# A small first load moved from Sync's queue to ScalarE's, in a decode kernel of attention and a gated feed-forward

## Chip, cores and metric

The kernel runs on one core of one Trainium2 chip. The metric is the device time of one execution in microseconds (us).

## What is computed

Two tokens (B = 2) of width 512 pass through a layer norm. Its result feeds a sliding-window attention over a cache (32 heads of width 128, the last 2,048 of 8,192 positions) and a gated feed-forward of width 1,376 without a nonlinearity. Both are added to the input. The reference, cut:

```python
def _A_ref(x, k_cache, v_cache, wq, wo):          # W = 2048, Sk = 8192
    q = (x @ wq).reshape(B, 1, 32, 128).transpose(0, 2, 1, 3)
    k, v = k_cache[:, :, Sk - W:, :], v_cache[:, :, Sk - W:, :]
    p = softmax(einsum("bhqd,bhkd->bhqk", q, k) * 128 ** -0.5)
    o = einsum("bhqk,bhkd->bhqd", p, v)
    return o.transpose(0, 2, 1, 3).reshape(B, 1, 4096) @ wo
def _B_ref(x, w_gate, w_up, w_down):
    return ((x @ w_gate) * (x @ w_up)) @ w_down
xn = layernorm(x)
return x + _A_ref(xn, ...) + _B_ref(xn, ...)
```

All data is float32. Some 160 MB of cache and weights are read once per execution.

## The kernel before, in words

The host lays all weights and the used part of the cache out in one array, `stream`, in the order in which they are read. `blocks()` (its list ends with `out`) cuts this into a first small load, key `("f", 0)`, and the loads of the steps, key `("s", i)`. The small load holds the input `x`, two selection matrices `pick` and `rows`, and `w` 0, the columns of the query weights for head 0: 128 rows of 542 numbers. Load 0 holds the rest of the first four heads' query weights (`w` 1), K of heads 0, 1 and 2, and parts of later query weights. Load 1 holds the gate and up weights of the feed-forward and K of head 3; load 2 holds down weights, K of heads 4 and 5 and the first values V. Later loads hold K of one or two heads and V of heads some steps back.

Each step load goes into one of three slots of SBUF (`slots`, `BUFS` = 3). `pump()` (line 297) issues the next load whenever a slot is free, all of them on Sync's queue (`sp.dma_start`, line 316). It is called once before anything else, and then gives out the small load and loads 0, 1 and 2. After that `done()` (line 318) calls it when the last field of a slot has been used: load 3 follows when K of heads 0 to 2 and the weights beside it are used up, load 4 when load 1 is. After the first `pump()` Sync also issues `x_nat` (the input once more, for the last addition) and `carry` (a small matrix that is used near the end).

The small load is read first. VectorE (DVE), TensorE (PE) and ScalarE (ACT) make the layer norm of it: a sum, a matmul with `mean_w`, squares, a second sum and matmul, a square root on ScalarE, a reciprocal, the product `xn` and its copy over 128 columns, `xnb`. `project_first(0)` multiplies `xnb` with `w` 0 into `q_first`, the query of head 0, in the bank `tr`. `project_first(1)` does the same for heads 1 to 3 when load 0 has landed. Then the loop over the loads runs for each head `h`: `products(h)` multiplies K by the query on VectorE, in place; `sums(h)` adds up the products and gives K's slot back; `maxima`, `weights` and `reciprocals` make the softmax on VectorE, GpSimd and ScalarE; `values` multiplies by V on TensorE, and `project_o` and `down` add into one accumulator.

`Flow` records all operations in the order of the program and then writes them out, one list for each engine, with semaphores where one operation needs another. Engines run their lists in order. Every DMA has a semaphore of its own, which counts to 16. As `Flow.emit` records every operation, nearly all of them have one line, L243, in the profile, so tiles tell them apart: `first` is the small load, `step` the slots, `tr` and `q` the banks of the queries, `s` the scores.

Of the kernel before, what the change touches and what calls it, by code (L numbers as in the profile page):

```python
# [50 lines left out]
def pitch(fields):  # L51

    n = -(-sum(w for _, _, w in fields) // BLK)
    return (n | 1) * BLK
# [217 lines left out]
def sliding_attention_plus_glu_kernel(  # L272
# [7 lines left out]
    pe, dve, act, pl, sp = (flow.engine(unit) for unit in ("pe", "dve", "act", "pl", "sp"))  # L280
# [12 lines left out]
    tiles, used, left, got = {}, {}, {}, {}  # L293
# [3 lines left out]
    def pump():  # L297
        while todo:
            key, fields, at = todo[0]
            if key not in tiles:  # L300
                if key[0] == "f":
                    n = sum(w for _, _, w in fields)
                    tiles[key] = flow.tile([P, n], "first")
                elif not slots:
                    return
                else:
                    tiles[key] = slots.pop(0)
                used[key] = 0
            todo.pop(0)
            c0 = used[key]  # L310
            for kind, i, w in fields:
                got[kind, i] = (tiles[key][:, used[key] : used[key] + w], key)
                used[key] += w
            c1 = used[key]
            src = stream[at : at + P * pitch(fields)].rearrange("(p i) -> p i", p=P)
            sp.dma_start(tiles[key][:, c0:c1], src[:, : c1 - c0])

    def done(kind, i):
        _, key = got.pop((kind, i))
        left[key] -= 1  # L320
        if left[key] == 0 and key[0] != "f":
            slots.append(tiles.pop(key))
            pump()

    pump()
    xT = got["x", 0][0].rearrange("p (b c) -> p b c", b=B)
    pick = got["pick", 0][0].rearrange("p (r s b) -> p r s b", s=2, b=B)
# [494 lines left out]
```

## Time and profile before

| | |
|---|---|
| Median of 3 runs | 376.0 us (375.85 to 376.57) |
| Profiled execution, from its first to its last instruction (span) | 374.6 us |
| What the median has beyond that span | 1.4 us |
| HBM read | 159.47 MB, 426 GB/s over the span |
| Queue of the loads (q1) | 3,938 packets, 159.54 MB |
| Instruction queues (q8, q14) | 12 packets, 0.16 MB |
| TensorE, VectorE, ScalarE, GpSimd busy | 248.4, 295.1, 58.1, 25.3 us |

The page gives no other time of the profiled execution than its span; the runs that were timed are separate executions. The span begins with the first instruction that the profile shows and ends with the last. "DMA share" is the mean busy share of the core's 16 DMA engines. In windows a DMA packet is counted whole where it starts, so a window that is short beside a packet (some 2.3 us for a row of a large load) can show a share of nothing or of more than one. The time "to landing" of a DMA runs from its issue to the moment when the last of its 16 parts has arrived.

### The profile page before, as it was taken

The numbers are of one execution on the slowest core, as the hardware profiler recorded it, in microseconds if no ns is written. First come the engines' busy times: TensorE is split into PE (matmuls) and PEld (weight loads), VectorE is DVE, ScalarE is ACT, GpSimd is POOL, SyncE is SP. The second block draws the span as 40 slices with busy tenths as digits, with TensorE's granted clock in tenths as the row PEclk, the third lists the DMA queues.
The fourth block names the chain that finished last, engine by engine and source line by source line (L and its number), as shares of the span: only waits on it lengthen the run. The fifth ranks groups of instructions, "written<-read, shape, count | busy, mean of one in ns | idle before, by whom it ended". The sixth has DMA issues, their size and how long they took to land.

```text
span 374.6 us, 2741 instructions
## 1 busy us (share of the span) xinstructions
PE 248.4 (66%) x1094; PEld 86.8 (23%) x1094; DVE 295.1 (79%) x147; ACT 58.1 (16%) x259; POOL 25.3 (7%) x78
## 2 busy tenths in 40 slices
PE   3167675896578157855658585781488647476997
PEld 3033124231132013211212121320122112111344
DVE  3069998994599994599999945999999459999760
ACT  1002012111022012110202020300121201111232
POOL 1000000100001000000000000010001000000010
PEclk9759695898689758896969886998689868666999
DMA  8999999999999999999999999999999999999996
GB/s 345 420 465 454 450 432 435 434 434 424 427 427 434 434 434 434 436 434 441 434 435 429 434 434 434 434 429 434 434 435 434 429 434 434 428 426 416 414 432 250
DMA packets 3950, 159.70 MB, mean 426 GB/s; under 512 B 466, under 2 KB 610, under 8 KB 994
## 3 DMA queue, kind: packets, MB, share of 16 engines
q1 hardware_dynamic: 3938, 159.54, 98.6%
q8 instruction: 8, 0.13, 0.1%
q14 instruction: 4, 0.03, 0.0%
HBM read 159.47 MB, written 0.07 MB: 426 GB/s over the span
## 4 chain that ended last, share of the span: by engine, by line
DMA 64%; DVE 26%; PE 7%; ACT 1%; issue 0%; SPq 0%
DMA step<-in_stream_dram 64%; DVE s L243 13%; DVE step L243 13%; PE q L243 3%; PE acc L243 2%; PE o_ps L243 2%; PE tr L243 1%; ACT o_sb L243 0%; DVE m L243 0%; ACT oT L243 0%; DVE rec L243 0%; SPq L243 0%; DVE o_out L243 0%
## 5 line engine op out<-in xcount | busy, mean ns | idle before, releaser
L243 DVE TENSOR_TENSOR step<-step,q 128x4096 f32<-128x4096 f32 x31 | 136.8, 4411 | 47.0 <-DMA step<-in_stream_dram 47.0
L243 DVE TENSOR_REDUCE s<-step 128x32 f32<-128x4096 f32 x32 | 141.4, 4419 | 1.1
L243 PE MATMUL q<-step,xnb 128*128 128x512 f32 (+1 forms) x128 | 79.0, 759 | 80.5 <-DMA step<-in_stream_dram 80.5
L243 PE MATMUL o_ps<-step,p 128*16 128x512 f32 (+1 forms) x512 | 98.5, 730 | 11.2 <-DMA step<-in_stream_dram 11.2
L243 PEld LDWEIGHTS q<-step,xnb 128*128 128x128 f32 x128 | 28.0, 238 | 123.5 <-DMA step<-in_stream_dram 92.9
L243 PE MATMUL acc<-step,oT 128*9 128x512 f32 (+1 forms) x88 | 39.1, 604 | 8.7 <-ACT oT L243 8.7
L243 PE MATMUL tr<-first,o_sb 128*128 128x2 f32 (+2 forms) x198 | 29.1, 266 | 17.9 <-ACT o_sb L243 12.0
L243 PEld LDWEIGHTS tr<-first,o_sb 128*128 128x128 f32 x198 | 26.8, 205 | 40.6 <-ACT o_sb L243 31.3
L243 PEld LDWEIGHTS o_ps<-step,p 128*16 128x16 f32 x512 | 17.6, 107 | 78.6 <-issue 64.9
L243 ACT COPY o_sb<-o_ps 128x512 f32<-128x512 f32 (+1 forms) x24 | 13.8, 576 | 121.4 <-PE o_ps L243 121.4
L243 POOL PARTITION_ALL_REDUCE mm<-m x32 | 11.3, 355 | 268.6 <-DVE m L243 258.7
L243 ACT ACTIVATE nm<-mm 128x2 f32<-128x2 f32 x32 | 6.5, 203 | 148.0 <-POOL mm L243 148.0
L243 ACT ACTIVATE p<-s,nm 128x16 f32<-128x16 f32 x64 | 19.2, 300 | 1.0
L243 POOL PARTITION_ALL_REDUCE sum<-rs x32 | 12.7, 398 | 69.1 <-ACT p L243 69.1
L243 ACT ACTIVATE oT<-tr,rec 128x1 f32<-128x1 f32 x64 | 12.2, 260 | 27.0 <-PE tr L243 27.0
L243 DVE TENSOR_TENSOR step<-step,tr 128x4096 f32<-128x4096 f32 x1 | 4.4, 4422 | 14.8 <-DMA step<-in_stream_dram 14.8
L243 ACT ACTIVATION_READ_ACCUMULATOR p<-s,nm 128x1 f32 x64 | 11.9, 187 | 0.0
L243 PE MATMUL o_ps<-step,xn 128*2 128x512 f32 (+1 forms) x48 | 10.1, 548 | 0.0
L243 PEld LDWEIGHTS acc<-step,oT 128*9 128x9 f32 x88 | 4.6, 94 | 21.1 <-ACT oT L243 14.5
L243 DVE TENSOR_TENSOR o_out<-acc,x_nat 128x128 f32<-128x128 f32 x1 | 0.3, 292 | 8.4 <-PE acc L243 8.4
L243 DVE TENSOR_REDUCE m<-s 128x2 f32<-128x32 f32 x32 | 6.0, 186 | 1.1
L243 DVE RECIPROCAL rec<-sum 128x2 f32<-128x2 f32 x32 | 5.0, 155 | 1.9 <-POOL sum L243 1.9
(43 smaller groups left out, 41.5 us busy)
## 6 DMA issues: line engine op xcount, KB each, us to landing
step<-in_stream_dram SPq DMA_DIRECT2D x14, 7936.0 KB, 37.7
step<-in_stream_dram SPq DMA_DIRECT2D x2, 7680.0 KB, 32.0
step<-in_stream_dram SPq DMA_DIRECT2D x1, 7872.0 KB, 58.2
step<-in_stream_dram SPq DMA_DIRECT2D x1, 7808.0 KB, 38.8
step<-in_stream_dram SPq DMA_DIRECT2D x1, 4864.0 KB, 30.3
step<-in_stream_dram SPq DMA_DIRECT2D x2, 2304.0 KB, 19.6
step<-in_stream_dram SPq DMA_DIRECT2D x1, 2048.0 KB, 18.3
step<-in_stream_dram SPq DMA_DIRECT2D x1, 1024.0 KB, 19.8
```

What stands on the lines that cost most here:

```text
L243: made = getattr(eng, method)(*args, **kwargs)
```

## The change

In `pump()` the queue of a load is chosen by its key: the small load goes to ScalarE's queue (`act`), all others stay on Sync's.

```diff
             c1 = used[key]
             src = stream[at : at + P * pitch(fields)].rearrange("(p i) -> p i", p=P)
-            sp.dma_start(tiles[key][:, c0:c1], src[:, : c1 - c0])
+            queue = act if key[0] == "f" else sp
+            queue.dma_start(tiles[key][:, c0:c1], src[:, : c1 - c0])
```

Nothing else is changed. The small load is the first thing that the program writes for ScalarE, and load 0 is now the first thing that it writes for Sync. Tiles, sizes, semaphores and the order of all later work are as before.

## The prediction

> **What bounds the kernel now.** I read the page first: the busy shares, the slices of DMA and the chain of waits.
>
> ```profile
> span 374.6 us, 2741 instructions
> PE 248.4 (66%) x1094; PEld 86.8 (23%) x1094; DVE 295.1 (79%) x147; ACT 58.1 (16%) x259; POOL 25.3 (7%) x78
> DMA  8999999999999999999999999999999999999996
> DMA 64%; DVE 26%; PE 7%; ACT 1%; issue 0%; SPq 0%
> ```
>
> The DMA engines are in their top tenth from the second slice to the last but one. Whether that means "always full" is read from their share in long windows (columns: stretch, length, five engines, granted clock, DMA share, GB/s):
>
> ```profile
> 100.00:200.00 100.00, 65.47 (x255) 19.46 (x254) 87.64 (x38) 15.31 (x70) 6.77 (x18) 0.80 1.00 435
> 200.00:300.00 100.00, 65.61 (x266) 20.40 (x266) 82.14 (x39) 16.23 (x78) 7.53 (x20) 0.85 1.00 435
> ```
>
> The share is 1.00 at 435 GB/s. So the stream of loads sets the end, and the 26% that the chain gives to DVE lies beside full queues. A change matters here in two ways only: it moves the moment at which the big loads begin on the DMA engines, or it makes the engines lose time later. The start is where the change is:
>
> ```profile
> 0.72 1.28 ACT L243 ACT_TABLE_LOAD   x1 [0.72 <-PEq L804]
> 0.72 0.37 SPq L243 DMA_DIRECT2D first<-in_stream_dram  x1
> 1.15 1.37 SPq L243 DMA_DIRECT2D step<-in_stream_dram  x3
> 3.55 0.16 DVE L243 TENSOR_REDUCE st<-first 128x2 f32<-128x8 f32 x1 [0.74 <-DMA first<-in_stream_dram]
> 5.62 0.26 ACT L243 ACTIVATE st<-tr,eps_t 128x2 f32<-128x2 f32 x1 [3.62 <-PE tr L243]
> 7.07 3.42 PE L243 MATMUL tr<-first,xnb 128*128 128x128 f32 x16 [1.48 <-DVE xnb L243]
> 21.98 4.42 DVE L243 TENSOR_TENSOR step<-step,tr 128x4096 f32<-128x4096 f32 x1 [14.81 <-DMA step<-in_stream_dram]
> ```
>
> SP hands out the small load at 0.72 and load 0 (the K of heads 0 to 2) at 1.15. The small load is used from 3.55; layer norm and the first query are done at 7.07 + 3.42 = 10.49, and DVE then waits until 21.98 for load 0. That wait of 14.81 us is the cover for whatever happens to the small load.
>
> **The change part by part.** *The issue.* Load 0 is given out at 0.72 instead of 1.15, 0.43 us earlier, and loads 1 and 2, x_nat and carry move up with it. What this is worth depends on when the DMA engines turn to load 0. The windows and slices around that moment (40 slices of 0.99 us in the first line):
>
> ```profile
> GB/s 0 350 263 0 88 526 0 0 88 88 175 0 0 175 88 0 0 263 0 88 0 0 88 175 0 0 350 350 350 350 263 526 175 175 788 350 263 526 613 88
> 1.70:2.69 0.99, 0.00 (x0) 0.00 (x0) 0.88 (x3) 0.30 (x1) 0.08 (x3) 1.00 0.79 191
> 2.69:3.18 0.49, 0.00 (x0) 0.00 (x0) 0.11 (x1) 0.00 (x0) 0.00 (x0) 1.00 5.53 2188
> 5.10:5.80 0.70, 0.49 (x2) 0.40 (x2) 0.00 (x0) 0.18 (x1) 0.00 (x0) 1.00 3.25 1404
> ```
>
> A packet is booked where it starts. The small load's first packets appear in the second slice of 1.70 to 2.69, at 1.73, 1.0 us after their issue. Load 0's first 16, one for each engine, start in 2.69 to 3.18, on average at about 2.93; their issue at 1.15 plus the same 1.0 us would have allowed 2.15, so they queue behind the small load, not behind SP. The engines thus spend 2.93 - 1.73 = 1.20 us on a load of 271 KB (its row stands below), which at 435 GB/s takes 0.64 us. The other 0.56 us is the first packets' slow start. If load 0 comes first, the 0.64 us of bytes is still to be moved; the 0.56 us is gained in full if load 0's long packets hide the slow start, and not at all if load 0 suffers it itself. Gain: 0 to 0.56 us, and I take the middle, 0.28, as no row leans either way.
>
> *Two queues on the same engines.* The small load is 128 rows of 271 KB / 128 = 2,168 bytes, 8 for each of the 16 engines, now on ScalarE's queue while SP's queue is full of long packets. One load on one queue never shows what such alternation costs; the nearest rows are the few instruction packets that cut into the stream. Each row is one packet in a window of 0.02 us (first two) or 0.01 us, so its share times window times 16 is its time:
>
> ```profile
> q8 instruction: 1, 0.02, 290.0%
> q1 hardware_dynamic: 1, 0.06, 884.7%
> q14 instruction: 1, 0.01, 193.1%
> q1 hardware_dynamic: 1, 0.06, 1620.0%
> q1 hardware_dynamic: 1, 0.06, 1463.8%
> ```
>
> In order: the 16 KB packet at 51.43 (0.93 us), the load packet behind it at 52.35 (2.83 us), the 8 KB packet at 86.42 (0.31 us), the load packet behind it (2.59 us), and an undisturbed neighbour at 86.75 (2.34 us). The big cut cost 0.93 + 2.83 - 2.34 = 1.42 us for bytes that at 27.2 GB/s per engine (435 / 16) need 0.60: 0.82 us lost. The small one cost 0.31 + 2.59 - 2.34 = 0.56 for 0.30: 0.26 us lost. For 2,168 bytes the loss lies between nothing and 0.82 us, eight times over: 0 to 6.6 us. I take the row nearest in size, the 8 KB one, and scale by bytes, 0.26 x 2,168 / 8,192 = 0.07 us, because the loss grew with the packet: 8 x 0.07 = 0.55 us. A loss below nothing is excluded: engines at share 1.00 have no idle time that the alternation could fill.
>
> *The small load lands later.* The cut at 51.43 also shows how the queues take turns, for it falls in the middle of load 2 (between its start after the landing of load 1 and its own landing):
>
> ```profile
> step<-in_stream_dram SPq DMA_DIRECT2D x1, 7872.0 KB, 58.2
> step<-in_stream_dram SPq DMA_DIRECT2D x1, 7808.0 KB, 38.8
> step<-in_stream_dram SPq DMA_DIRECT2D x1, 7680.0 KB, 20.8
> first<-in_stream_dram SPq DMA_DIRECT2D x1, 271.0 KB, 2.8
> ```
>
> So a second queue gets its turn between two packets of one load. With turns one for one, each of the 8 small packets waits for one long one: 3.25 x 0.70 = 2.28 us (the window 5.10 to 5.80), plus 0.08 for its own bytes and the 0.07 above, 2.43 us; eight of them from 1.73 end at 21.2, landed by 21.5. From there to the first query it takes 10.49 - 3.55 = 6.94 us, so DVE's first product starts at 28.4 instead of 21.98, 6.5 us late. The next thing that could be late is load 3, which needs load 0's slot; then load 4, which needs load 1's:
>
> ```profile
> 48.95 0.36 SPq L243 DMA_DIRECT2D step<-in_stream_dram  x1
> 58.02 0.33 SPq L243 DMA_DIRECT2D step<-in_stream_dram  x1
> ```
>
> DVE frees the slot 48.95 - 21.98 = 26.97 us after its first product: now at 55.4, with packets 1.0 us later at 56.4. The engines run out of loads 0 to 2 (23,360 KB, 55.0 us at 435 GB/s, from 2.93) at 57.9. That leaves 1.5 us, so the lateness costs nothing; load 4 would be issued at 64.5, with a whole load still ahead of it. If that cover were gone, every us more would be a us of the end.
>
> *The rest.* ScalarE's table load (1.28 us) moves behind an issue of 0.37 us and ends near 2.4, long before 5.62: nothing, and 0.4 us of an already covered chain if it were not. No wait is added. x_nat and carry stay behind loads 0 to 2 and are used at the end. The last loads and what follows them are untouched.
>
> **Sum.** 374.6 - 0.28 + 0.55 = 374.9 us of span. The runs' median is 376.0, 1.4 us above the profiled span, and I keep that difference: **376.3 us**. The case's own range takes a gain of 0 to 0.56 and a loss of 0 to 1.0 us: 375.4 to 377.0. A measurement of this kernel tells about 0.2%, 0.75 us, from no change, so this case reads as "same".
>
> **The rivals.** *Every turn costs a full bubble (slower).* If the loss is a fixed time for each change of queue and not in proportion to bytes, eight turns cost 8 x 0.26 = 2.1 to 8 x 0.82 = 6.6 us on every engine: 376.0 - 0.28 + 2.1 = 377.8 to 382.3, the low end likelier because the 8 KB row is nearer. It decides from (0.75 + 0.28) / 8 = 0.13 us a turn. For it: both cuts cost more than their bytes. Against it: those packets go somewhere other than a load's do, the losses differ threefold, and successive loads on SP's queue show a share of 1.00.
>
> *Load 3 comes too late (slower).* If the small load's completion waits for a ninth long packet, it lands at 23.9, the slot is free at 57.8, packets come at 58.8, and the engines stand empty for 0.9 us; slower matrix work in the chain would add to that. 377.0 to 378. For it: only 1.5 us of slack. Against it: the fastest engine has the least slack, the others more.
>
> *The small load goes in one turn.* Then the engines change queue once instead of eight times, and the sum is 376.0 - 0.28 + 0.07 = 375.8, with the landing either near 3 or near 20 us. The cut in mid-load speaks against long turns of SP's queue, though not against long turns of short packets. The Trainium skill, in "DMA: Bandwidth & Descriptors", section "Queues, rings and completion order", says that an engine goes round its queues and drains a whole packet, typically 9 to 17 descriptors, before it switches; by that rule the eight would go together, and the cut in mid-load agrees with it only if a packet here holds fewer than eight long descriptors.
>
> *The small load is free (faster).* If its packets fit beside the long ones at no cost, load 0 starts 1.20 us earlier: 374.8. Against it: share 1.00 leaves no room beside.
>
> *The small load is not first on ScalarE.* If the table load stays ahead, its issue comes at 2.0 instead of 0.72, it lands later by about one turn, and load 0 still goes first. The slack above is mostly used; 376.0 to 376.6.
>
> **How the numbers follow.** Forecast 0.45, the bubble 0.20, one turn 0.15, free 0.10, load 3 late 0.07, table load first 0.03. Faster by over 0.2%: the free case and the edge of one turn, 0.13. Slower: the bubble, most of load 3 late, the edge of the forecast, 0.29. The rest, 0.58, is within. The range leaves out the upper half of the bubble and part of the free case: 375.1 to 378.2.
>
> **What would show it.** Right: load 0's packets near 1.73, the small load landing near 21, DVE's first product near 28, load 3 issued near 55 with the DMA share still 1.00 around 58, an end within 0.75 us. Wrong: load 0's packets of more than 2.4 us all through the first 20 us (bubbles), a window below 1.00 at 57 to 60 (load 3), or a small load that lands near 3 (no alternation), which would make the middle of the argument wrong even if the time holds.

## The result, and the profile after

The changed kernel takes 378.41 us (median of 5 runs, 377.88 to 378.80) against 376.26 us (375.85 to 376.57, 5 runs) before: a ratio of 1.0055 with a 95% interval of 1.0044 to 1.0066. It is 2.1 us slower, where 376.3 us and "no change" had been forecast, with a range of 375.1 to 378.2. The profiled execution of the changed kernel took 378.04 us with a span of 376.7.

The page's head, its DMA line and its queues:

```profile
span 376.7 us, 2741 instructions
DMA  8999999999999999999999999999999999999994
q1 hardware_dynamic: 3794, 159.26, 98.1%
q10 hardware_dynamic: 144, 0.28, 0.2%
```

The stream of loads is still what bounds the kernel; the small load has moved to a queue of its own, q10. The timeline of the start:

```profile
0.72 0.40 ACTq L243 DMA_DIRECT2D first<-in_stream_dram  x1
0.72 1.32 SPq L243 DMA_DIRECT2D step<-in_stream_dram  x3
1.15 1.28 ACT L243 ACT_TABLE_LOAD   x1 [1.15 <-PEq L805]
22.39 0.16 DVE L243 TENSOR_REDUCE st<-first 128x2 f32<-128x8 f32 x1 [19.59 <-DMA first<-in_stream_dram]
25.90 3.78 PE L243 MATMUL tr<-first,xnb 128*128 128x128 f32 x16 [1.48 <-DVE xnb L243]
29.80 4.42 DVE L243 TENSOR_TENSOR step<-step,tr 128x4096 f32<-128x4096 f32 x1 [3.80 <-PE tr L243]
```

The change does what it says: both loads are given out at 0.72, the table load follows. But the small load is first used at 22.39 instead of 3.55, and VectorE's first product starts at 29.80 instead of 21.98. The two loads' times from issue to landing:

```profile
step<-in_stream_dram SPq DMA_DIRECT2D x1, 7680.0 KB, 21.5
first<-in_stream_dram ACTq DMA_DIRECT2D x1, 271.0 KB, 21.6
```

Load 0 was given out 0.43 us earlier and took 0.7 us longer, so it lands at 22.2, some 0.3 us later than before. The later issues on Sync's queue:

```profile
56.77 0.36 SPq L243 DMA_DIRECT2D step<-in_stream_dram  x1
375.12 0.35 SPq L243 DMA_DIRECT2D out_dram<-o_out  x1
```

Load 3 is issued at 56.77 instead of 48.95. The output of the kernel before left at this time:

```profile
373.05 0.35 SPq L243 DMA_DIRECT2D out_dram<-o_out  x1
```

So 2.07 us are lost before the output leaves, and what follows is as it was. The last stretch of the DMA engines shows in which form, in 40 slices of 0.2 us from 367 to 375 us, first before, then after:

```profile
GB/s 328 369 533 287 492 389 348 471 348 451 492 369 369 410 328 338 287 246 225 225 205 205 133 51 10 0 0 0 0 0 0 0 0 0 90 236 3 0 0 0
```

```profile
GB/s 492 573 123 492 492 328 492 389 287 492 471 328 451 399 379 389 420 440 256 348 287 184 225 205 154 82 61 61 31 72 41 41 20 31 10 0 0 0 0 0
```

Before, the loads end at 372.0 (the later traffic is the output). After, the rate is down to about half (some 200 GB/s) from 371.2 instead of 370.6, and from 372.0 on 10 to 82 GB/s go on until 374.0. At 27 GB/s for one engine (435 / 16) that is one to three engines which are late; most are later by less than one us.

### The profile page after: what moved, and what is told of

Its sections match the earlier page's. It is cut to its first block, busy times and chain, and to the rows that moved or that the text cites. A ratio compares the mean times of both kernels' runs of the same rounds, so it can differ in the third digit from the quotient of the medians.

```text
span 376.7 us, 2741 instructions
## 1 busy us (share of the span) xinstructions
PE 246.4 (65%) x1094; PEld 86.2 (23%) x1094; DVE 294.9 (78%) x147; ACT 58.0 (15%) x259; POOL 25.4 (7%) x78
## 4 chain that ended last, share of the span: by engine, by line
DMA 53%; PE 28%; DVE 14%; ACT 2%; issue 2%; DVEq 0%; SPq 0%
DMA step<-in_stream_dram 47%; PE o_ps L243 10%; DVE step L243 7%; PE q L243 7%; PE tr L243 6%; DVE s L243 6%; PE acc L243 6%; DMA first<-in_stream_dram 6%; ACT o_sb L243 1%; ACT oT L243 1%; DVE m L243 0%; DVE xnb L243 0%; ACT hT L243 0%; DVE o_sb L243 0%; DVE st L243 0%
## 5 line engine op out<-in xcount | busy, mean ns | idle before, releaser
L243 PE MATMUL q<-step,xnb 128*128 128x512 f32 (+1 forms) x128 | 76.2, 738 | 56.0 <-DMA step<-in_stream_dram 56.0
L243 PEld LDWEIGHTS q<-step,xnb 128*128 128x128 f32 x128 | 26.8, 227 | 97.6 <-DMA step<-in_stream_dram 65.3
L243 PE MATMUL acc<-step,oT 128*9 128x512 f32 (+1 forms) x88 | 37.3, 583 | 8.7 <-ACT oT L243 8.7
L243 PE MATMUL tr<-st,mean_w 128*128 128x2 f32 x4 | 1.2, 362 | 23.3 <-DVE st L243 23.3
```

The source lines that it names most:

```text
L243: made = getattr(eng, method)(*args, **kwargs)
```

## The experiments

Theory A: load 3 comes too late. The small load waits for its turns and lands late, VectorE frees load 0's slot late, and the DMA engines run out of work near 58 us. Theory B: the turns of the two queues in the first 20 us cost the 2 us. In all ratios below the kernel before, run beside each, is 1.

**Load 3 in two pieces.** The changed kernel, with the part of load 3 that goes where K of heads 0 and 1 were given out earlier (the body of `early()` is cut):

```diff
+EARLY = CQ - NC * DH + 2 * (CK + CP)                       # 10,752 columns
+            if key == ("s", 3):                              # in pump()
+                sp.dma_start(tiles[key][:, EARLY:c1], src[:, EARLY : c1 - c0])
+                continue
             sums(h)
+            if h == 1:
+                early()      # sp.dma_start(slot of load 0[:, :EARLY], load 3[:, :EARLY])
```

> The changed kernel, with load 3 given out in two pieces: the first 10,752 of its 15,872 columns as soon as K of heads 0 and 1 is used up (about 47.8 us), the rest at 56.8 as before. Theory A (load 3 is issued too late, because the small load lands at 22.4 instead of 3.5 and DVE frees its slot at 56.77 instead of 48.95, so the DMA engines run empty near 58): the loss goes, 376.0 to 376.7 us, and no load packet that starts at 58 to 60 takes over 2.4 us. Theory B (the turns of the two queues in the first 20 us cost the 2 us): stays at 378.0 to 378.8.

376.24 us, ratio 0.9998 (0.9990 to 1.0007). Its timeline:

```profile
22.36 0.16 DVE L244 TENSOR_REDUCE st<-first 128x2 f32<-128x8 f32 x1 [19.56 <-DMA first<-in_stream_dram]
29.78 4.42 DVE L244 TENSOR_TENSOR step<-step,tr 128x4096 f32<-128x4096 f32 x1 [3.79 <-PE tr L244]
56.74 0.33 SPq L244 DMA_DIRECT2D step<-in_stream_dram  x1
```

Everything that the change did is still there, with the small load and the first product as late as in the changed kernel; only the engines have a piece of load 3 (issued at 47.68) when they finish load 2. Its first packets, of 43,008 bytes, take 1.59 us each, which is the rate of the stream (27.1 GB/s for one engine). The whole loss is gone. All turns of the two queues are still there too. That is theory A, and it excludes B.

**Lateness without a second queue.** The kernel before, with added sums on VectorE between the landing of load 0 and the first product. Nobody reads them. This is the edit with 57 groups; the others differ in the list alone:

```diff
+    late, at = flow.tile([P, 96], "late"), 0
+    for n in [12, 12, 12, 12, 9]:                            # 57 groups of 128
+        w1 = got["w", 1][0][:, : n * DH].rearrange("p (n d) -> p n d", d=DH)
+        dve.tensor_reduce(late[:, at : at + n], w1, axis=AX.X, op=ALU.add)
+        at += n
```

> The kernel before, with about 8 us of added VectorE work (sums over query weights that nobody reads) between the landing of load 0 and the first product, so that load 3 is issued near 57.0 although the small load goes first on Sync's queue. Theory A: as slow as the changed kernel, 378.0 to 378.8 us, with long first packets of load 3. Theory B: no queue changes, so 376.0 to 376.6.

> The same with about 5 us of added VectorE work: load 3 is issued near 54.0, some 4 us before the first engine runs out. Theory A: still covered, 376.0 to 376.6 us. If lateness costs something before the engines run out (a theory C: the lateness hurts later, by the work of heads 3 to 5, not by load 3), 377 or more. Theory B: 376.0 to 376.6.

> The same with about 10 us of added VectorE work: load 3 is issued near 59.0, after the engines have run out. Theory A: every further us of lateness costs a us, so about 2.2 us above the kernel with 8 us added: 380.2 to 380.8. Theory B: 376.0 to 376.6. Theory C: slower, but with less than a us for a us.

> The kernel before with 45 instead of 57 groups of added VectorE sums, so that load 3 is issued near 55.4, the time that the prediction gave for the change. Theory A, as the prediction had it (1.0 us from issue to packets, engines empty from 58.0): 1.5 us to spare, 376.0 to 376.6 us. Theory A with a longer way from issue to the last engine (up to 3 us, as in the changed kernel): a few engines are late by some tenths, 376.3 to 377.0.

> The same with 51 groups: load 3 issued near 56.4, between the kernel that lost nothing (54.0) and the changed one (56.8). With 1.0 us from issue to packets the first packets come at 57.4, before any engine is empty: 376.0 to 376.6 us. With the longer way: 377.0 to 378.4.

Measured, in the order of load 3's issue:

| kernel | load 3 issued, us | median, us | ratio (95% interval) |
|---|---|---|---|
| before | 48.95 | 376.02 to 376.26 | 1 |
| 36 groups (5 us) | 54.03 | 376.12 | 0.9999 (0.9990 to 1.0008) |
| 45 groups (6 us) | 55.16 | 376.29 | 1.0004 (0.9996 to 1.0013) |
| 51 groups (7 us) | 56.11 | 377.43 | 1.0033 (1.0020 to 1.0045) |
| the changed kernel | 56.77 | 378.41 | 1.0055 (1.0044 to 1.0066) |
| 57 groups (8 us) | 57.29 | 378.00 | 1.0046 (1.0034 to 1.0058) |
| 72 groups (10 us) | 58.87 | 378.58 | 1.0062 (1.0050 to 1.0074) |

With 57 groups no second queue is used, and the kernel is as slow as the changed one: lateness alone is enough. With 36 and 45 groups nothing is lost, so theory C is out up to there. Between 55.16 and 56.11 the loss sets in, although no engine has read all of load 2 before 57.97. What happens there is seen in load 3's first packets. Each row is a short window in which one long packet of load 3 starts, and up to four tiny ones; share times window times 16 is their time together. In the kernel with 45 groups, 58.07 to 58.09:

```profile
q1 hardware_dynamic: 3, 0.06, 743.1%
```

That is 2.38 us, of which the tiny packets have some hundredths: an undisturbed load packet, as 14 of the 16 first ones are in this kernel; the other two take 2.42 and 2.68 us. In the kernel with 51 groups (its profiled execution took 378.01 us, 0.6 above its median), 58.13 to 58.15, 58.77 to 58.79 and 60.22 to 60.24:

```profile
q1 hardware_dynamic: 5, 0.06, 1156.6%
q1 hardware_dynamic: 1, 0.06, 1140.9%
q1 hardware_dynamic: 1, 0.06, 993.8%
```

3.70 and 3.65 us: first packets that start 2.0 and 2.7 us after the issue take 1.3 us longer. The third row takes 3.18 us and starts 4.1 us after the issue; another starts at 60.04. All engines but one (59.84) are through with load 2 by 58.72, so two engines have stood without work for 1.3 us or more. In the changed kernel, 58.07 to 58.09 and 59.78 to 59.79 (0.01 us):

```profile
q1 hardware_dynamic: 2, 0.06, 925.0%
q1 hardware_dynamic: 1, 0.06, 2051.2%
```

2.96 and 3.28 us, and the second starts 3.0 us after the issue at 56.77. In this kernel load 2 ends on the first engine at 58.04, on 15 of the 16 by 58.85 and on the last at 59.98, so the engine that starts at 59.78 had stood without work for at least 0.9 us. In these kernels nothing is lost when load 3 is issued 2.8 us before the first engine is through with load 2 (55.16 to 57.97), and 1.2 us are lost with 2.0 (56.11 to 58.09). A slack counted with 1.0 us is too short.

The last kernel of the table was a miss: with 1.6 us more lateness than with 57 groups, 2.2 us more were expected and 0.6 us came. "Slower, but with less than a us for a us" is what theory C had said of it, though C is excluded as a cause by the kernels that lost nothing and by load 3 in two pieces. The landing of load 3's last part says why the step is small. The issues, each with its time from issue to landing, with 57 groups (issued at 57.29) and with 72 (at 58.87):

```profile
step<-in_stream_dram SPq DMA_DIRECT2D x1, 7936.0 KB, 22.9
```

```profile
step<-in_stream_dram SPq DMA_DIRECT2D x1, 7936.0 KB, 21.4
```

The last engine is done at 80.2 and 80.3. With 57 groups one engine is very late (its last row of load 3 ends at 79.85) and the others less (77.7 to 78.6); with 72 all but one are empty when the load comes, their first packets start 1.0 to 2.0 us after the issue (59.84 to 60.86), and all end load 3 at 79.2 to 80.0. The slowest engine, which sets the end, hardly differs.

**The turns alone.** The kernel before, with a second copy of 408 columns of the small load, of which only `pick` is read (near 60 us), given out on ScalarE's queue at about 6 us; and the same copy on Sync's queue ahead of load 0. The main lines of both edits:

```diff
+    pick = again[:, B * NC : B * NC + 8 * B].rearrange("p (r s b) -> p r s b", s=2, b=B)
     act.activation(st[:, 2, :], tr[:, 8 : 8 + B], AF.Sqrt, bias=eps_t)
+    act.dma_start(again, again_src)                          # on ScalarE's queue, or
+            if key[0] == "f":                                # in pump(), on Sync's
+                sp.dma_start(again, again_src)
```

> The kernel before, with a second copy of 408 of the 542 columns of the small load, given out on ScalarE's queue at about 6 us, while load 0 runs; only the selection matrix is read from it, at about 60 us, so nothing is late. It isolates the turns of two queues. Its bytes take 0.21 MB / 435 GB/s = 0.5 us. Theory A (load 3 too late; turns cost only bytes): 376.5 to 377.0 us, the same as with the copy on Sync's queue within 0.4. Theory B (bubbles at each turn): 378.3 or more, 2 us above the copy on Sync's queue.

> The same copy on Sync's queue between the small load and load 0, so that it has no turns: both theories 376.5 to 377.0 us. It is what the copy on ScalarE's queue is compared with.

On ScalarE's queue 376.80 us, ratio 1.0016 (1.0007 to 1.0025): 0.6 us (0.3 to 0.9), with 0.5 us for the bytes alone. The turns cost little or nothing beyond their bytes. On Sync's queue 378.90 us, ratio 1.0075 (1.0062 to 1.0089). That is a miss by 2 us for both theories: of the two copies, the one without turns is the slow one. The landing of load 0, on Sync's (issued at 1.62) and then on ScalarE's (1.14):

```profile
step<-in_stream_dram SPq DMA_DIRECT2D x1, 7680.0 KB, 23.3
```

```profile
step<-in_stream_dram SPq DMA_DIRECT2D x1, 7680.0 KB, 21.3
```

Load 0 lands at 24.9 against 22.4, so the loss is there from the start. The window 4.40 to 5.50 of the kernel with the copy on Sync's queue has room for a packet of load 0 on few engines only:

```profile
4.40:5.50 1.10, 0.57 (x2) 0.50 (x2) 0.41 (x3) 0.00 (x0) 0.00 (x0) 1.00 0.38 112
```

It starts two long packets (112 GB/s x 1.10 us = 0.12 MB), the first ones of load 0 on two engines that turn to it about 1.7 us after most others (3.4 to 3.6). That looks like load 3's case, a load whose first packets come late on some engines. But the kernel before gives load 0 out only 1.5 us before its first engine is through with the small load (1.15 to 2.69), and there no engine waits for it. So the time that a load needs ahead is not one fixed figure; what makes the difference between these two kernels was not tried.

**Sync a little later.** The changed kernel, with `x_nat` and `carry` ahead of load 0:

```diff
+    sp.dma_start(x_nat[::RB, :], x_rows)
+    sp.dma_start(carry, carry_rows)
     pump()
```

> The changed kernel, with x_nat and carry given out on Sync's queue ahead of load 0, which is then issued near 2 us instead of 0.72. The small load stays on ScalarE's queue but meets no long packet at first. Theory A: it lands near 3.5 to 5, load 3 is issued near 49, 376.0 to 377.0 us (load 0 may start 0.3 us later than in the kernel before). A theory D, that the use of ScalarE's queue as such costs 2 us: 378 or more. Theory B: between, as the turns are few.

377.35 us, ratio 1.0033 (1.0021 to 1.0046): above what A expected and below D. Its small load and its load 0, with the latter issued at 2.23:

```profile
step<-in_stream_dram SPq DMA_DIRECT2D x1, 7680.0 KB, 21.3
first<-in_stream_dram ACTq DMA_DIRECT2D x1, 271.0 KB, 2.8
```

The small load lands early again, from ScalarE's queue, so the queue as such is not slow. Load 3 is issued at 50.48, early enough. Load 0 lands at 23.5 instead of 21.95, 1.6 us later, which would be enough for the 1.25 us: with Sync's issue at 2.23 instead of 1.15 its first packets start at 3.2 to 4.7 instead of 2.7 to 3.2. No run separated this, so it is argued, not shown.

**Turns with short packets.** The changed kernel, with load 0 in two DMAs, the first with its 1,536 columns of query weights:

```diff
+            if key == ("s", 0):
+                w1 = fields[0][2]
+                sp.dma_start(tiles[key][:, :w1], src[:, :w1])
+                sp.dma_start(tiles[key][:, w1:c1], src[:, w1:c1])
+                continue
```

> The changed kernel, with load 0 in two DMAs on Sync's queue: first its 1,536 columns of query weights (rows of 6 KB, 0.23 us for a packet), then the rest. The small load's 8 packets for each engine now take turns with 8 short packets, so it lands near 5 us instead of 22.4. Theory A: load 3 in time, 375.6 to 376.5 us, the gain of the earlier start of load 0 if there is one. Theory B: as many turns as in the changed kernel, 378.0 to 378.8.

376.30 us, ratio 1.0007 (0.9998 to 1.0016). The loads' times to landing:

```profile
step<-in_stream_dram SPq DMA_DIRECT2D x1, 6912.0 KB, 21.1
step<-in_stream_dram SPq DMA_DIRECT2D x1, 768.0 KB, 5.3
first<-in_stream_dram ACTq DMA_DIRECT2D x1, 271.0 KB, 5.5
```

The same number of turns, with short packets, lets the small load land at 6.2 and load 3 go out at 49.30, and the loss is gone. It also shows that nothing is to be gained here: with the lateness removed, the earlier issue of load 0 leaves the time where it was, in this kernel as in the one with load 3 in two pieces. No version beats the kernel before.

## Why the prediction was wrong

**What bounds the kernel** was right: the stream of loads sets the end, and the change acts through it alone.

**The issue** was taken at 0.28 us gained. The first 16 packets of load 0, in the window 1.70 to 2.60 of the changed kernel:

```profile
1.70:2.60 0.90, 0.00 (x0) 0.00 (x0) 0.79 (x3) 0.73 (x1) 0.08 (x3) 1.00 3.36 1092
```

They start at 1.73 and later (the last at 2.18), as forecast, and take 3.36 x 0.90 = 3.02 us each instead of 2.27. Load 0 suffers the slow start itself, the lower end that the prediction had given. The Trainium skill ("DMA: Bandwidth & Descriptors", section "Issuing engines are not separate DMA queues") says that giving out DMAs from several engines saves only the time of the issue; here not even those 0.43 us arrived.

**The turns** were taken at 0.55 us lost in bubbles, with up to 6.6 us as a bound and a rival at 0.20. One round of turns in the changed kernel, 4.50 to 5.50, by queue:

```profile
q1 hardware_dynamic: 16, 0.98, 226.7%
q10 hardware_dynamic: 16, 0.03, 9.5%
```

A long packet takes 2.267 us, as without a neighbour, and a small one 0.095 us. There is no bubble, and the instruction packets were no guide to this price. That the two wrong terms nearly give what came is luck: together they made load 0 0.27 us later, and it lands some 0.3 us later. That each engine takes turns, one long packet to one small, was right. The Trainium skill (same page, section "Queues, rings and completion order") has an engine drain a packet of typically 9 to 17 descriptors in its turn; in this trace a turn was one row of one load, and the eight small rows did not go together. Of how many descriptors a row is made, the trace does not show.

**The step that failed** is "That leaves 1.5 us, so the lateness costs nothing". It counted the slack with 1.0 us from issue to packets, the time of the first packet at the kernel's start. By that rule even the issue at 56.77 that was measured would have cost nothing: packets at 57.8, engines empty from 57.9. The runs showed in its place that load 3 has to go out more than 2.0 us before the first engine is through with load 2: 55.16 lost nothing, 56.11 lost 1.2 us, 56.77 lost 2.1. The 1.0 us holds for the first engine alone. The last engine that had to wait got its first packet 2.0 us after the issue where nearly all were empty (72 groups), 3.0 in the changed kernel and 4.1 with 51 groups, and first packets took up to 1.5 us longer than later ones.

The lateness itself was forecast too small as well, 55.4 instead of 56.77. VectorE's 26.97 us from the first product to the free slot were right. The small load landed at 22.3 instead of 21.5: the slow first packet (0.75 us) and the later start of the last engine (0.45 us) had been left out, and eight turns without bubbles gave some 0.5 us back. The chain from landing to first product took 29.80 - 22.39 = 7.41 instead of 6.94 us, mostly by the matmuls of the first query, 3.78 against 3.42. The kernel with 45 groups suggests that the forecast issue time would just have been early enough. So it took both errors: an issue 1.4 us later than forecast, and a margin of 0.7 us at most (55.4 to 56.11) where 1.5 had been counted.

The rival "Load 3 comes too late" was the case, at a chance of 0.07 and a price of 377.0 to 378 us. Its condition was not: the small load did not wait for a ninth long packet, and did not land at 23.9. The sign that the prediction named for it, a DMA share below 1.00 from 57 to 60, cannot tell: the share is 0.89 in the changed kernel and 0.85 in the kernel before, as a packet is counted whole where it starts.

**The price.** Load 3's last part lands 0.8 us later than before (56.77 + 23.0 = 79.8 against 48.95 + 30.0 = 79.0), but the end is 2.1 us later. The trace does not name the engine of a packet, but the packets can be strung together by their times: in the stream each begins within 0.04 us of the end of the one ahead of it on its engine, and each engine reads 8 rows of every load. Strung so, the 3,200 rows of the step loads fall on 16 engines with 200 rows each, before and after.

In the changed kernel one engine is through with load 2 by 58.82, starts load 3 at 59.78, takes 3.28 us for its first row instead of 2.34, and ends load 3 at 79.46. In the kernel before, the latest engine that has met no instruction packet by then ends load 2 at 58.66 and load 3 at 77.40, 2.06 us earlier. The late engine makes none of this good. It meets one of the eight 16 KB instruction packets too (at 154.4; 1.42 us in the prediction's working) and is the last of all, at 373.96. Before, the last two engines had met one such packet each and ended at 371.87 and 371.89. So the whole price is what one engine lost at load 3.

Part of the price is chance: in the kernel before, the changed one and those with added sums, eight of the 16 engines meet a 16 KB packet, one each, and the other eight none. With 51 groups the engine that is latest at the end of load 3 (79.79) meets none and ends at 372.85; another (79.44) meets one and ends last, at 373.91.

## What to carry to other kernels

In this kernel a small load beside a large one, on another queue of the same DMA engines, landed when the large one did: each of its rows waited for a row of the other. Before moving it, count its rows per engine times the other's time per row, follow the lateness to the next load that needs a freed buffer, and look how long before the engines run out that load is issued. Here 2.8 us were enough and 2.0 were not, and the kernel's own start shows that the figure is not the same everywhere, so it is worth a run with added idle work like those above. If it must share, give it short rows to share with, or give out the piece of the next load whose space is free early.

## What the runs showed of the hardware that was not expected

- Two queues with loads into SBUF alternated row by row without loss: 2.27 us for 61,440 bytes and 0.09 for 2,168 in every round after the first long packet.
- A load that found its engines out of work, or nearly so, started slowly: many of its first packets took 2.5 to 3.8 us instead of 2.34, and the last engine that waited got its first 2.0 to 4.1 us after the issue. From 55.16 to 56.11 us of issue time, for a queue that ends from 58.0 on, the loss went from nothing to 1.2 us.
- Lateness beyond that cost little more: with load 3 issued 1.6 us later (57 to 72 groups), the time rose by 0.6 us.
- No engine took over rows of a late one: each read its 200 rows, and the latest set the end.
